# Gated linear attention and a spatial gating unit on one core: keys and queries of three batches turned on VectorE and placed through HBM

## The chip, the cores and the metric

The kernel runs on one core of one Trainium2 chip. The metric is the device time in microseconds of one execution. The engines are TensorE (PE, with its weight loads PEld), VectorE (DVE), ScalarE (ACT), GpSimd (POOL) and SyncE (SP), which issues all the transfers of this kernel in one queue, in order.

## The reference

For 4 batches, 8 heads, 768 steps and head dimension 48, gated linear attention keeps a state per head. Its output, heads side by side (width 384), is the input of a gated MLP with a spatial gating unit:

```
f = sigmoid(f_logit)
for t in range(768):
    state = f[t][:, None] * state + outer(k[t], v[t])
    y[t] = q[t] @ state
h = gelu_tanh(x @ w_in)            # x = y, 384 -> 1024
u, v = split(h)                    # 512 each
v_n = (v - mean) / sqrt(var + 1e-6) * g_ln
v_s = w_sg @ v_n + b_sg            # over the 768 steps
out = x + (u * v_s) @ w_out        # 512 -> 384
```

All in float32.

## The kernel before, in words

The 768 steps of a batch are cut into 6 tiles of 128 steps (24 tiles over all, `N`, numbered n; batch 0 is tiles 0 to 5), and a tile into two chunks of 64. Within a chunk attention is done by products, between chunks by the state.

The steps of one tile are named in the kernel by a short name and the tile's number:

- `f`, `k`, `q`, `v`: loads, 192 KB each. Keys and queries go to `kqs` (three buffers), each head padded from 48 to 64 columns (`HD`), so that two heads stand at partitions 0 and 64 after a transpose.
- `e`, `l`, `lh`, `ll`, `cum`, `up`, `dn`: the gates' logarithms, their running sums by a matmul, and the exponentials of both signs. `mq` and `mk` multiply queries and keys with them (L529, L525) on VectorE or GpSimd.
- `do`, `di`: the decay of a whole chunk is brought to columns; for tiles 6 and up by way of a scratch in HBM, `dec_d` (L532, L536).
- `tr`: eight TensorE transposes (L559), one for each pair of heads of keys and of queries, into two PSUM banks; `tc` copies them to `sks` (two buffers), on ScalarE as a rule (L566, recorded at the helper's line L321).
- `su`: score products (L578) and state products keys x values (L583); `ms` masks the scores into `sts` (L588); `sa`, `sm` add to the state and decay it (L604, L607).
- `y`: output products (L626), masked scores with values and queries with the state; `ty`, `jy` take them out (L630, L634).
- `xT`: transposes of the attention's output (L655), `xh`, `xl` split it into a high and a low float32r part. `hv`, `hu`, `sg`, `po` are the matmuls of the MLP, all recorded at L650, each product as three float32r matmuls.

`su` and `y` use the array in quadrants (64 x 64), the others the whole array.

The order on all engines is written out ahead by a planner (`Plan`): a greedy schedule with a cost for each step (`T`), a queue and wire time for each transfer (`W`), rings of buffers (`RINGS`), due times for TensorE's steps, and a list of shifts of due times and choices of engine (`MOVES`). The due times lay the attention of batch b among the spatial gating and projection of batch b - 1, between the fractions `A0` and `A1` of that work; in batch 0 they follow the arrival of the loads. `op`, `pe` and `dma` add a step with what it needs. Up to 45 us the planner fills TensorE's gaps with matmuls of zeros (L992).

Of the kernel before, what the change touches and what calls it, by code (L numbers as in the profile page):

```python
# [64 lines left out]
cs:-20.3 wain0:23.1 wfin0:0:POOL wfin1:0:POOL wfin2:0:DVE wbin3:74.5 wcin3:-16 wrin4:6 wcin4:-2.5 wdin4:248.6  # L65
wfin4:0:POOL ldin5:-27.6 ldin6:19.5 wfin6:55.2 ldin7:-0.2 wrin7:-173.7 wdin7:-33.2 ldout0:1.4 wpout0:8.4 wdout0:-20.4
ldout1:102.8 waout1:-4.7 wl0.1:734.5 ldsg1:15.1 wl1.0:243.5 wT1.1:-1.1 ldsg2:1.8 wT3.0:-1.8 wT4.0:172.6 wl4.0:-28.9
wT4.1:25.4 ldsg5:-33.2 wT5.0:-378.9 v0:2.1 w0.0:0:POOL mk0:0:POOL sz0:-389.4 sa0.0:-15.5 nl0:435.6 po0:292 f1:-417.7
k1:-526.9 q1:-48.1 w1.0:0:POOL w1.1:0:POOL do1:-7.7 ms1:-73.4 sa1.0:-14.4 sm1.0:0:POOL hv1:322.3 ns1:41 nl1:4.4
f2:-1.5 k2:8.6 v2:110.2 w2.0:0:POOL w2.1:-23.4 mq2:-141.7 di2:0:ACT tc2.0:-20.1 tc2.1:-3.7 ms2:-0.6 xl2:-8.7  # L70
sg0.0:84.4 sm_0.0:27.1 hu0.1:-291 sm_0.2:0:POOL gu0.3:-6 sg0.3:153.3 sb0.3:18.6 sm_0.3:0:POOL mq3:-138.3 sm3.0:0:POOL
y3:5.2 po3:746.4 f4:31.3 tc4.0:0:DVE sm4.0:-216.6 sm4.1:0:POOL q5:1.6 w5.0:-108.7 w5.1:-57.1 dn5:244.4 mk5:0:POOL
su5:-1.6 ms5:-0.3 sm5.0:0:POOL sm_1.0:0:POOL hu1.1:6.3 hu1.2:-0.2 gu1.2:-85 hu1.3:391.7 sm_1.3:0:POOL w6.1:-178.4
dn6:140.6 mk6:0:POOL sm6.1:0:POOL xT6:-11.5 k7:-2.9 ll7:145.8 up7:0.7 mq7:0:POOL mk7:0:POOL tc7.0:0:DVE xT7:-40.9
nd7:25 po7:995.4 ll8:-42:POOL mq8:-53.5:POOL xT8:-25.9 hv8:-20.6 sg2.2:34.6 mq9:0:POOL y9:-1 po9:951.5 lh10:-86.2
ll10:0:POOL y10:-287.3 f11:52.3 tc11.1:0:DVE hv11:66.2 sg3.0:1549 sg3.1:1637.5 sg3.3:10.9 po11:59.2 dn13:6.1
mq14:0:POOL mk14:0:POOL tr14:9.8 sm14.1:41.5 hv14:103.6 hu4.1:99.7 sg4.2:188 po14:645.7 f15:-2.9 lh15:-38.6
tc15.1:0:DVE po15:14.5 f17:-49.9 lh17:-27.7 mq17:0:POOL tr17:-130.7 hu5.0:-128.5 sg5.0:1269.4 sg5.1:150.6
sm_5.1:0:POOL sg5.2:295.4 po17:945.8 cum18:-26.7 up18:35.6 mq18:0:POOL y18:-129.1 ty18:-18.6 ll19:0:POOL mq19:0:POOL
# [212 lines left out]
def gla_moe_kernel(ctx: ExitStack, tc: tile.TileContext, q, k, v, f, w_in, g_ln, w_sg, b_sg, w_out, cst, out):  # L292
# [230 lines left out]
    def mul_k(n, e):  # L523
        kt = kqs[n % NQ][:, 0, :, 0:D]
        ENG[e].tensor_mul(kt, kt, f_raw.pop(n))  # L525

    def mul_q(n, e):
        qt = kqs[n % NQ][:, 1, :, 0:D]
        ENG[e].tensor_mul(qt, qt, eb_of[n][:, :, 0:D])  # L529
# [41 lines left out]
    def scores(n):  # L571

        kq, sk, vs = kqs[n % NQ], sks[n % NS], vss[n % NV]
        last = n % NT == NT - 1
        for p in range(NP):
            for par, c in ((0, 0), (1, 1), (0, 1), (1, 0)):
                r = feat(par)
                nc.tensor.matmul(ps_s[rows(score_rows(c, 2 * p + par)), par, p * C : (p + 1) * C], sk[r, 0, p, c], sk[r, 1, p, c], start=True, stop=True)  # L578
            for c, par in ((0, 0), (1, 1), (0, 1), (1, 0)):
                if c == 1 and last:  # L580
                    continue
                h = 2 * p + par
                nc.tensor.matmul(  # L583
                    ps_s[rows(par), c, 256 + p * D : 256 + (p + 1) * D], kq[rows(c), 0, h, :], vs[rows(c), h], start=True, stop=True
                )
# [523 lines left out]
```

## Time and profile before

| | |
|---|---|
| time, three runs | 382.89, 384.6 (median), 385.07 us |
| span of the profiled execution | 380.6 us |
| own time of the profiled execution | not on the page; the runs are 2.3 to 4.5 us above its span |
| instructions | 11390 |
| TensorE busy | 369.6 us (97%), 4808 matmuls |
| weight loads busy | 341.5 us (90%) |
| VectorE busy | 233.6 us (61%) |
| ScalarE busy | 213.2 us (56%) |
| GpSimd busy | 55.9 us (15%) |
| DMA queue of the program | 31.35 MB in 123476 packets, 39.8% of 16 engines' span |
| eight transposes of a tile (L559) | 273 ns median each, pipelined |

A span runs from the first instruction to the last; the time is some microseconds longer. Busy time counts an engine's instructions; matmuls are pipelined, so TensorE's busy time does not say that it is at its peak. The chain of work that ended last is followed back from the last instruction through what released it. A wait is put down to what came last of all that an instruction needed.

### The profile page before, as it was taken

The page shows a single profiled execution, that of the slowest core. Times are in us where ns is not written, and L with a number is a line of the kernel's source. Part 1 is how long each engine was busy: PE and PEld are TensorE (multiplying, and loading weights), DVE is VectorE, ACT ScalarE, POOL GpSimd, SP SyncE. Part 2 cuts the span into 40 slices and gives each one's busy share as a digit, 9 for nine tenths or more (in the row PEclk, how much of TensorE's full clock was granted, in tenths as well). Part 3 has the DMA queues.
Part 4 walks back from the last instruction along what each step waited for, and adds up shares of the span by engine and source line. Part 5 has one row for each costly group of instructions (what it writes and reads, how often), then busy time and mean ns, then how long its engine had stood idle before and what let it go on. Part 6 is the DMA issues. An engine that isn't in the chain of part 4 may idle for free.

```text
span 380.6 us, 11390 instructions
## 1 busy us (share of the span) xinstructions
PE 369.6 (97%) x4808; PEld 341.5 (90%) x4808; DVE 233.6 (61%) x544; ACT 213.2 (56%) x483; POOL 55.9 (15%) x97
## 2 busy tenths in 40 slices
PE   8999999999999999999999999999989999999992
PEld 3777988999998898999999998999979998999991
DVE  3599998689578764247769635266656644254531
ACT  4677769637565957647447647678343554811100
POOL 1211453012341011100201110132000100200000
PEclk9999999999999999999999999999999999999998
DMA  8989998200285951002476622012244110000021
GB/s 178 219 231 233 223 215 202 72 14 0 45 145 90 198 99 22 22 21 39 94 144 109 106 66 41 22 21 45 44 106 85 22 46 2 2 21 2 0 83 49
DMA packets 123533, 32.13 MB, mean 84 GB/s; under 512 B 115797, under 2 KB 122069, under 8 KB 123477
## 3 DMA queue, kind: packets, MB, share of 16 engines
q1 hardware_dynamic: 123476, 31.35, 39.8%
q8 instruction: 39, 0.64, 0.8%
q14 instruction: 18, 0.14, 0.1%
HBM read 26.57 MB, written 4.77 MB: 82 GB/s over the span
## 4 chain that ended last, share of the span: by engine, by line
PE 96%; DMA 1%; DVE 1%; ACT 0%; issue 0%; SPq 0%
PE ps_b L650 67%; PE ps_y L626 6%; PE ps_b L559 6%; PE ps_s L578 4%; PE ps_b L992 3%; PE ps_s L583 2%; PE ps_b L655 2%; PE ps_b L508 1%; PE ps_b L444 1%; PE ps_b L511 1%; PE ps_b L544 1%; DMA gg<-in_moe_w_in_dram 1%; PE ps_b L512 1%; DVE tmp L768 0%; ACT u L393 0%
## 5 line engine op out<-in xcount | busy, mean ns | idle before, releaser
L650 PE MATMUL ps_b<-w_sg_hi,vh 128*128 128x384 f32 x192 | 65.3, 340 | 0.0
L650 PE MATMUL ps_b<-w_sg_hi,vh_lo 128*128 128x384 f32 x192 | 64.9, 338 | 0.0
L650 PE MATMUL ps_b<-w_sg_lo,vh 128*128 128x384 f32 x192 | 64.8, 338 | 0.0
L650 PE MATMUL ps_b<-w_out_hi,gg 128*128 128x384 f32 x174 | 48.0, 338 | 0.0
L737 DVE SCALAR_TENSOR_TENSOR tmp<-ps_b,cols,b_bc 128x384 f32<-128x384 f32 x32 | 19.7, 615 | 29.5 <-PE ps_b L650 25.0
L650 PEld LDWEIGHTS ps_b<-w_sg_hi,vh 128*128 128x128 f32 x192 | 36.1, 188 | 0.2
L650 PEld LDWEIGHTS ps_b<-w_sg_lo,vh 128*128 128x128 f32 x192 | 36.1, 188 | 0.0
L650 PEld LDWEIGHTS ps_b<-w_sg_hi,vh_lo 128*128 128x128 f32 x192 | 36.0, 188 | 0.0
L321 ACT COPY sk<-ps_b 112x512 f32<-112x512 f32 x44 | 24.6, 589 | 14.2 <-PE ps_b L559 8.0
L650 PEld LDWEIGHTS ps_b<-w_out_hi,gg 128*128 128x128 f32 x174 | 31.8, 188 | 0.1
L650 PE MATMUL ps_b<-xTh,w_in_hi 128*128 128x384 f32 x84 | 29.2, 348 | 0.0
L650 PE MATMUL ps_b<-w_out_lo,gg 128*128 128x384 f32 x87 | 29.1, 335 | 0.0
L710 DVE SCALAR_TENSOR_TENSOR vh_lo<-vg,vg_rs,vh 128x512 fp32r<-128x512 f32 x24 | 18.0, 749 | 17.1 <-ACT vh L705 17.1
L650 PE MATMUL ps_b<-xTl,w_in_hi 128*128 128x384 f32 x84 | 28.4, 338 | 0.0
L650 PE MATMUL ps_b<-xTh,w_in_lo 128*128 128x384 f32 x84 | 28.4, 338 | 0.0
L753 ACT CAST gg<-tmp 128x384 fp32r<-128x384 f32 x29 | 14.5, 510 | 23.3 <-DVE tmp L742 20.6
L316 ACT ACTIVATE f<-f 128x384 f32<-128x384 f32 x48 | 24.8, 524 | 4.6 <-DMA f<-in_f_logit_dram 4.1
L559 PE MATMUL ps_b<-cs,kq 128*112 128x128 f32 x192 | 25.5, 275 | 1.9 <-DVE kq L525 1.5
L626 PE MATMUL ps_y<-vs,st 64*64 64x48 f32 x768 | 27.2, 219 | 0.0
L626 PE MATMUL ps_y<-S,sk 48*64 48x48 f32 x768 | 27.0, 219 | 0.0
L626 PEld LDWEIGHTS ps_y<-vs,st 64*64 64x64 f32 x768 | 24.7, 134 | 2.0 <-issue 1.4
L650 PE MATMUL ps_b<-w_in_hi,xTh 128*128 128x512 f32 x63 | 26.2, 416 | 0.0
...
## 6 DMA issues: line engine op xcount, KB each, us to landing
f<-in_f_logit_dram SPq DMA_DIRECT2D x24, 192.0 KB, 3.7
kq<-in_k_dram SPq DMA_DIRECT2D x24, 192.0 KB, 4.0
kq<-in_q_dram SPq DMA_DIRECT2D x24, 192.0 KB, 5.9
vs<-in_v_dram SPq DMA_DIRECT2D x24, 192.0 KB, 4.5
out_dram<-tmp SPq DMA_DIRECT2D x24, 192.0 KB, 1.9
...
```

Of the source, the lines that this page charges most:

```text
L316: nc.scalar.activation(dst, src, func, **kw)
L321: (nc.scalar.copy if e == "ACT" else ENG[e].tensor_copy)(dst, src)
L559: nc.tensor.transpose(psum[f"tr{n}"][j][:W2, p * P : (p + 1) * P], kq[:, j, 2 * p : 2 * p + 2, :].rearrange("t h d -> t (h d)")[:, :W2], i ...
L578: nc.tensor.matmul(ps_s[rows(score_rows(c, 2 * p + par)), par, p * C : (p + 1) * C], sk[r, 0, p, c], sk[r, 1, p, c], start=True, stop=True)
L583: nc.tensor.matmul(ps_s[rows(par), c, 256 + p * D : 256 + (p + 1) * D], kq[rows(c), 0, h, :], vs[rows(c), h], start=True, stop=True)
L626: nc.tensor.matmul(ps_y[rows(c), half, h * D : (h + 1) * D], a, m, start=start, stop=stop)
L650: nc.tensor.matmul(ps, a, m, start=(j == 0), stop=(j == len(seq) - 1))
L655: nc.tensor.transpose(ps[:, j], x_sb[n][:, j * P : (j + 1) * P], ident)
L710: nc.vector.scalar_tensor_tensor(vl, v_raw.pop(n), rs, vh.bitcast(F32), op0=ALU.mult, op1=ALU.subtract)
L737: nc.vector.scalar_tensor_tensor(t, psum[f"sg{g}.{ft}"][:, :E], g_col[:, ft : ft + 1], b_bc[:, tokens(g)], op0=ALU.mult, op1=ALU.add)
L753: nc.scalar.copy(gt[(g, ft)][0], g_raw[(g, ft)])
L992: steps = plan.warm(plan.run(), 45.0, lambda k, n: nc.tensor.matmul(ps_b[k][:, : n * P], zeros, zeros[:, None, :].to_broadcast((P, n, P)), ...
```

## The change

For batches 1 to 3 (tiles 6 to 23) `tr` and `tc` go. In their place:

- `tt`, three for each tile: VectorE turns 32 x 32 blocks of the scaled keys and queries (`turn_kq`), 128 steps x 8 (key or query, pair of heads) x 32 columns, and writes 8 values side by side for each time.
- `to`, three for each tile: a store of 128 KB to a scratch in HBM, `kq_d`, pieces of 1 KB (`turned_out`).
- `ti`, two for each tile: a read of 192 KB back to 48 partitions each, 4 KB to a partition (`turned_in`).

Keys and queries of these tiles are stored without the padding. The layout of `sks` is the same for all tiles now, [feature, time, key or query, pair], so that neighbouring times are 8 values apart; batch 0 keeps `tr` and `tc`, and the copy writes in this layout. The state products of all tiles load 48 columns of the keys and not 64; the rows between are cleared once (`zs`). `sts` has one buffer, not two, so that `ms` needs `y` of the tile before. `y` stands ahead of the next tile's `su` in the due times, and `A0`, `A1` and `MOVES` are others.

```diff
+BL = 32
+NBL = 2 * D // BL
-A0, A1 = 0.25, 0.75
+A0, A1 = 0.1, 0.8
...
-    sks = [cp.tile([P, 2, NP, 2, C], F32, name=f"sk{i}") for i in range(NS)]
-    sts = [cp.tile([P, 2, NP, C], F32, name=f"st{i}") for i in range(NS)]
+    sks = [cp.tile([P, P, 2, NP], F32, name=f"sk{i}") for i in range(NS)]
+    sts = [cp.tile([P, 2, NP, C], F32, name="st")]
...
+    kq_d = dp.tile([N, 2, D, P // BL, BL, 2 * NP], F32, name="kq_d")
...
+    def kq_of(n):
+        t = kqs[n % NQ]
+        if n < NT:
+            return t[:, :, :, 0:D]
+        return t.rearrange("t j h d -> t (j h d)")[:, : 2 * E].rearrange("t (j h d) -> t j h d", j=2, d=D)
...
     def trans_copy(n, j, e):
-        copy(e, sks[n % NS][:W2, j].rearrange("d p c t -> d (p c t)"), psum[f"tr{n}"][j][:W2])
+        copy(e, sks[n % NS][:W2, :, j].rearrange("d t p -> d p t"), psum[f"tr{n}"][j][:W2].rearrange("d (p t) -> d p t", p=NP))
+    def turn_kq(n, m):
+        t = tt_of[n, m] = buf("tt", [P, BL, 2 * NP], F32)
+        blocks = kq_of(n).rearrange("t j (p x) d -> t (j p) (x d)", x=2)[:, :, m * BL : (m + 1) * BL]
+        nc.vector.transpose(t.rearrange("r t a -> r a t"), blocks)
+    def turned_out(n, m, e):
+        dst = kq_d[n].rearrange("x d b t a -> (x d) b (t a)")[m * BL : (m + 1) * BL].rearrange("r b y -> b r y")
+        ENG[e].dma_start(dst, tt_of.pop((n, m)).rearrange("r t a -> r (t a)"))
+    def turned_in(n, par, e):
+        ENG[e].dma_start(sks[n % NS][feat(par)].rearrange("d t j p -> d (t j p)"), kq_d[n, par].rearrange("d b t a -> d (b t a)"))
...
-                nc.tensor.matmul(ps_s[rows(score_rows(c, 2 * p + par)), par, p * C : (p + 1) * C], sk[r, 0, p, c], sk[r, 1, p, c], start=True, stop=True)
+                nc.tensor.matmul(ps_s[rows(score_rows(c, 2 * p + par)), par, p * C : (p + 1) * C], sk[r, rows(c), 0, p], sk[r, rows(c), 1, p], start=True, stop=True)
...
-                    ps_s[rows(par), c, 256 + p * D : 256 + (p + 1) * D], kq[rows(c), 0, h, :], vs[rows(c), h], start=True, stop=True
+                    ps_s[feat(par), c, 256 + p * D : 256 + (p + 1) * D], kt[rows(c), h], vs[rows(c), h], start=True, stop=True
...
-                b_ = (sk[feat(par), 1, p, c], Sn[feat(par), c, p])
+                b_ = (sk[feat(par), rows(c), 1, p], Sn[feat(par), c, p])
...
-                att.append([f"su{m0 + i}"] + ([f"y{m0 + i - 1}"] if i else []) + ([f"tr{m0 + i + 1}"] if i + 1 < NT else []) + ([f"xT{m0 + i - 2}"] if 2 <= i < 2 + GR else []))
+                att.append(([f"y{m0 + i - 1}"] if i else []) + [f"su{m0 + i}"] + ([f"xT{m0 + i - 2}"] if 2 <= i < 2 + GR else []))
...
-            dma(f"{'kq'[j]}{n}", lambda e, n=n, j=j: load_kq(n, j, e), W["kq"[j]], ["clear", f"tr{n - NQ}", f"su{n - NQ}"])
+            dma(f"{'kq'[j]}{n}", lambda e, n=n, j=j: load_kq(n, j, e), W["kq"[j]], ["clear", f"tr{n - NQ}", f"su{n - NQ}"] + [f"tt{n - NQ}.{m}" for m in range(NBL)])
...
+        if early:
             pe(f"tr{n}", ...)
             ...
+        else:
+            for m in range(NBL):
+                op(f"tt{n}.{m}", lambda e, n=n, m=m: turn_kq(n, m), T["tt"], [f"mq{n}", f"mk{n}"], take=("tt",))
+                dma(f"to{n}.{m}", lambda e, n=n, m=m: turned_out(n, m, e), W["to"], [f"tt{n}.{m}"], free=[("tt", f"tt{n}.{m}", 0)])
+            for par in range(2):
+                dma(f"ti{n}.{par}", lambda e, n=n, par=par: turned_in(n, par, e), W["ti"], [f"to{n}.{m}" for m in range(par, par + 2)] + [f"su{n - NS}", f"y{n - NS}"])
-        op(f"ms{n}", lambda e, n=n: mask_scores(n), T["ms"], [f"su{n}", f"y{n - NS}"])
+        op(f"ms{n}", lambda e, n=n: mask_scores(n), T["ms"], [f"su{n}", f"y{n - 1}"])
```

More of the change, by code (lines that the diff above doesn't have):

```diff
@@ L36 @@
 CW = 128 + 128 + 64
-A0, A1 = 0.25, 0.75
+BL = 32
+NBL = 2 * D // BL
+A0, A1 = 0.1, 0.8
 T_FIRST, T_TILE, V_FIRST, V_TILE, T_SG = 16, 8, 22, 3.589, 43.931
 T = dict(
-    cum_c="DVE:0.2", clear="POOL:1.3", zy="DVE:0.6", wa="ACT:0.452", wb="DVE:0.268", wp="DVE:0.268", wq="DVE:0.468", wr="DVE:0.268", wc="DVE:0.468",
+    cum_c="DVE:0.2", clear="POOL:1.3", zy="DVE:0.6", zs="DVE:0.35", wa="ACT:0.452", wb="DVE:0.268", wp="DVE:0.268", wq="DVE:0.468", wr="DVE:0.268", wc="DVE:0.468",
     wd="DVE:0.468 POOL:1.0", we="ACT:0.403", wf="DVE:0.468 POOL:1.0", wh="ACT:0.362", wl="DVE:0.465", e="ACT:0.507", l="ACT:0.413",
@@ L64 @@
 MOVES = """
[L65 to L79, printed above, removed]
@@ L80 @@
-xT20:40 sg6.1:373.3 sg6.3:178.9 f21:-165.8 q21:158.4 w21.1:0:POOL xT21:-24.3 f22:-19.9 lh23:-172.2 ll23:0:POOL
-tr23:-429.2 sg7.1:48.1 hu7.2:-22.7 ok_s:683.9
+cs:-120.7 wdin0:287.6 wpin1:191.3 wdin1:-92.1:DVE wfin1:-77.8 wbin2:124.3 wdin2:366.9:DVE wfin2:0:POOL wbin3:515.4
+wdin4:-2.6:DVE ldin5:-396 ldin6:-63 wpin7:36 wdin7:5.6 wfin7:-97.2 wpout0:26.9 wdout0:-120.2:POOL waout1:136.4
+wpout1:-13.5 wdout1:3:POOL ldout2:-6.7 wrout2:0.9 wdout2:4.4 wfout2:-0.3:DVE wbout3:205.3 wcout3:80.9 wT0.0:-126.2
@@ new lines @@
+wh0.0:-328.1 wT0.1:147.4 ldsg1:4.4 wh1.0:-33.2 wT1.1:27.9 wT3.0:-96.6 wl3.0:102.9 ldsg5:102.8 wh5.1:-16.8
+w0.0:31.4:DVE w0.1:0:POOL mk0:1.6:POOL tc0.1:-31.6 sa0.0:3 sa0.1:202.6 xl0:78.4 po0:88.3 f1:-116.5 k1:-1185.7
+q1:-181.7 w1.0:-20.4 w1.1:34.2:DVE mk1:82.4:POOL di1:210.8 tc1.1:118.6:ACT ms1:-15.2 sm1.0:6.3:POOL ns1:-44.8 nl1:82.7
+f2:-5.6 w2.0:1.6 w2.1:-37.4 tc2.0:24.6 ms2:194.5 sm2.0:-1:DVE xl2:18.5 hv2:-106.5 hu0.0:-35.6 gu0.0:6.7 sm_0.0:-254.7
+sh0.0:-58.1 sg0.2:-39.3 hu0.3:-189.4 sb0.3:-43.2 sm_0.3:-241.8 w3.0:120.9 di3:0:ACT sa3.0:13.7 sa3.1:4.5 sm3.1:17.6
@@ new lines @@
+nq3:102 re3:-4.9 w4.0:44.5:DVE w4.1:15.2:DVE up4:-1.3 mq4:-25.1:DVE mk4:-4.2:DVE di4:-3.2 tc4.0:3.5:DVE tc4.1:118.9
+su4:-41.9 sa4.0:340.7 sm4.1:158.2 nh4:3.7 po4:-99.4 w5.1:1.3 cum5:12.5 mk5:250:DVE di5:-15.9:ACT ms5:70 sb1.0:297.5
+sm_1.0:-1.2:POOL sg1.1:72.9 sb1.1:-249.2 sm_1.1:36.1:POOL hu1.2:-177.8 sb1.2:178.3 sm_1.2:524.8 hu1.3:81.1 out5:18.7
+w6.0:-1.8:POOL lh6:0.4 mq6:-17.8:DVE mk6:28.7:POOL tt6.1:106 sa6.1:115.2 sm6.1:0:POOL w7.1:-122.2:POOL lh7:-109.9
+mq7:-202.8:DVE mk7:0:DVE tt7.0:54.1 tt7.1:-19.2 sm7.0:-14.7:DVE po7:859.3 w8.0:0:POOL w8.1:-15.6:DVE lh8:-257.5:ACT
@@ new lines @@
+mq8:-92.6:POOL mk8:0:POOL tt8.0:288.6 sa8.1:136 y8:137.4 jy8:23.1 sg2.1:123.2 sm_2.1:12.8 sl2.1:-42 sm_2.2:-505.6
+k9:-178.8 w9.0:-22.5 lh9:9.3 ll9:0:POOL to9.1:-3 sm9.0:-11.6 v10:-57.1 ll10:-67.4:DVE mq10:40.6 po10:221.2 f11:-64.1
+lh11:-75.6 ll11:-42.9:DVE mq11:-47.5 su11:-812.4 sm11.0:-35.4 sg3.0:1698.4 sg3.1:1877.7 sg3.3:75.6 w12.1:-23.7
+lh12:1.1:ACT w13.0:0:POOL lh13:0.8:DVE ll13:188.8:POOL mq13:135.3:POOL su13:0.7 sa13.0:21.3 ty13:4.9 xh13:0.2
+out13:2.5 w14.0:-123.7 lh14:8.5:DVE mq14:0.1:POOL mk14:30 tt14.1:-37.3 to14.2:63.3 hu4.1:313.1 sm_4.1:-16.2 gu4.2:-0.7
@@ new lines @@
+sb4.3:67 sl4.3:-106.4 po14:207.5 f15:8.6 ll15:189.9 mk15:-22.8:DVE di15.0:-0.1 tt15.1:53.4 w16.0:-7.4:POOL w16.1:155.9
+lh16:-73.8 ll16:126.4:DVE sm16.0:-19.5 y16:152.6 lh17:5.2:ACT ll17:-0.9 mq17:-31.8 tt17.1:-8.2 sg5.0:1142.6
+sm_5.0:123.9 sg5.1:-81.1 sm_5.1:-36.4:POOL sg5.2:692 hu5.3:-6.1 f18:-41.9 ll18:-1.2 mq18:0:DVE mk18:6.3:DVE mq19:-9.3
+ms19:-0.4 sm19.1:96.8:POOL hv19:430.1 ll20:41.3:POOL mq20:28.9 mk20:65.5:POOL su20:0.4 sm20.1:-11.3 jy20:-30.5
+xT20:89.4 hu6.0:137.4 sb6.0:19.3 sm_6.1:1.4 sg6.2:138.3 po20:-4.1 f21:290.5 lh21:0:DVE ll21:10.8:DVE
@@ L82 @@
+sm21.0:-228.3:POOL ty21:-0.5 nr21:-0.1 w22.0:1.8 lh22:0:ACT sm22.0:-7.7:DVE f23:-180.7 q23:4.4 w23.1:-32.9
+lh23:-4.2:ACT ll23:0:POOL do23:-111.8 di23.0:52.5 tt23.1:49.7 to23.1:-19.8 nh23:-10.7 sm_7.1:-94.6 sh7.3:-0.6
 """
@@ L523, in mul_k @@
     def mul_k(n, e):
[L524 removed]
+        kt = kq_of(n)[:, 0]
         ENG[e].tensor_mul(kt, kt, f_raw.pop(n))
     def mul_q(n, e):
[L528 removed]
+        qt = kq_of(n)[:, 1]
         ENG[e].tensor_mul(qt, qt, eb_of[n][:, :, 0:D])
@@ L875, in gla_moe_kernel @@
     op("zy", lambda e: nc.vector.memset(ps_y[:, :, 0:E], 0.0), T["zy"], ())
+    op("zs", lambda e: nc.vector.memset(ps_s[:, :, 256 : 256 + NP * D], 0.0), T["zs"], ())
     for kind, m in (("in", 8), ("out", 4)):
```

25 lines of the change are left out of this document (13 added, 12 removed).

## The prediction

> **What bounds the kernel now.** First the page's busy times and its chain of work that ended last.
>
> ```profile
> span 380.6 us, 11390 instructions
> PE 369.6 (97%) x4808; PEld 341.5 (90%) x4808; DVE 233.6 (61%) x544; ACT 213.2 (56%) x483; POOL 55.9 (15%) x97
> ...
> PE 96%; DMA 1%; DVE 1%; ACT 0%; issue 0%; SPq 0%
> PE ps_b L650 67%; PE ps_y L626 6%; PE ps_b L559 6%; PE ps_s L578 4%; PE ps_b L992 3%; PE ps_s L583 2%; PE ps_b L655 2%; PE ps_b L508 1%; PE ps_b L444 1%; PE ps_b L511 1%; PE ps_b L544 1%; DMA gg<-in_moe_w_in_dram 1%; PE ps_b L512 1%; DVE tmp L768 0%; ACT u L393 0%
> ```
>
> The chain lies on TensorE for 96% of the span; the transposes of keys and queries (L559) are 6% of it. An average hides stages, so second the busy times by stage: batch 0 with the weights up to 95 us, then one row for each of batches 1 to 3 (us, then PE, PEld, DVE, ACT, POOL, granted clock, DMA share, GB/s).
>
> ```profile
> 0.00:95.00 95.00, 92.91 (x1185) 79.16 (x1186) 76.72 (x191) 65.55 (x152) 23.21 (x41) 1.00 0.72 159
> 95.00:173.00 78.00, 78.00 (x1128) 73.29 (x1128) 46.44 (x107) 49.82 (x114) 14.09 (x22) 1.00 0.41 78
> 173.00:251.00 78.00, 78.00 (x1128) 73.47 (x1128) 45.88 (x108) 48.12 (x110) 7.73 (x16) 1.00 0.41 76
> 251.00:330.00 79.00, 77.46 (x1124) 72.64 (x1123) 44.68 (x101) 42.79 (x96) 10.16 (x16) 1.00 0.23 45
> ```
>
> In batches 1 to 3 TensorE is busy without a gap, at the full granted clock, while VectorE and ScalarE are some 60% busy and DMA 41% or less. So a microsecond of TensorE work removed there is a microsecond of time, as long as nothing else becomes late. Third, what TensorE waits for in the whole run (total, times, longest):
>
> ```profile
> PE ps_b L559 <- DVE kq L525: 1.5, 1, 1.5
> ...
> PEld ps_s L578 <- issue: 3.2, 15, 0.4
> PEld ps_b L559 <- DVE kq L525: 2.0, 1, 2.0
> ```
>
> One late operand of a transpose, 1.5 us, and otherwise almost nothing. Fourth, the chain in order of time within batch 1 (start, us, what), which prices one tile.
>
> ```profile
> by line: PE ps_b L650 71.7%; PE ps_y L626 7.9%; PE ps_b L559 7.1%; PE ps_s L578 4.7%; PE ps_s L583 3.0%; PE ps_b L655 2.5%; PE ps_b L511 1.9%; PE ps_b L512 1.4%
> ...
> 100.25 0.87 PE ps_b L559 x8
> ...
> 101.48 3.16 PE ps_b L650 x18
> 104.64 0.28 PE ps_s L578 x8
> ...
> 118.61 0.93 PE ps_y L626 x64
> 119.55 1.02 PE ps_b L559 x8
> ...
> 122.66 0.33 PE ps_b L655 x3
> ...
> 128.79 0.87 PE ps_b L559 x8
> 129.66 1.08 PE ps_y L626 x64
> 130.74 0.13 PE ps_s L578 x8
> ...
> 131.67 3.87 PE ps_b L650 x18
> ```
>
> A tile's eight transposes cost 0.87 us; the score and state products (L578, L583) 0.93 us (130.74 to 131.67); the output products (L626) 0.93 us. The 0.15 us more at 119.55 and at 129.66 is paid by whatever comes first after a switch between small and full matmuls. It stays with the neighbours, because the new order has as many visits to the small products (output of the last tile and scores of the next side by side) as the old one.
>
> **The change part by part.**
>
> *Transposes removed.* 18 tiles x 0.87 us = 15.7 us of TensorE, all in the stages without a gap. Check: 7.1% of 78 us is 5.5 us in batch 1, six tiles at 0.92, the excess being the switches. Gain taken 15.7, ends 14.2 (0.79 a tile, if the 0.08 at the end of a group also stays) and 16.6. The single 1.5 us wait belonged to such a transpose; its late key product is next needed by the VectorE turn, so I count no gain from it.
>
> *State products load 48 columns.* In the 0.93 us of scores each of four array quadrants takes 16 weight loads of 64 columns, 58 ns each; the transposes of x (L655) take 0.33 us for three loads of 128 columns, 110 ns each. The line through both gives 45 ns for 48 columns, so 13 ns x 8 loads = 0.10 us a tile. Batches 1 to 3 have 15 full tiles and three with half the state products: 16.5 x 0.10 = 1.7 us. Batch 0's 0.6 us I leave out, since TensorE still waits for loads and runs filler matmuls (L992) there. Ends: 0, if the pace of 128 instructions in 0.93 us binds rather than the columns, and 2.3.
>
> *The turned tile is read with a stride.* Its layout goes from time innermost to eight values between neighbouring times, 32 bytes apart, for all 24 tiles. Half of the weight loads of the scores and half of those of the outputs read it so: 16 loads per quadrant and tile. The trace of before has no such read by TensorE. Lower end: nothing. Upper end: a strided load takes as long as one of twice the columns, 110 ns for 58, or 52 ns x 16 = 0.83 us a tile, 14.9 us over 18 tiles and 19.8 over 24. The nearest rows are two reads by ScalarE, of every second word and of a contiguous tile:
>
> ```profile
> L321 ACT COPY sk<-ps_b 112x512 f32<-112x512 f32 x44 | 24.6, 589 | 14.2 <-PE ps_b L559 8.0 <-PE ps_y L626 3.1 <-PE ps_s L578 3.0
> ...
> L604 DVE TENSOR_TENSOR S<-S,ps_s 112x192 f32<-112x192 f32 x40 | 14.0, 349 | 7.4 <-PE ps_s L583 6.4 <-POOL S L607 0.4
> ...
> L753 ACT CAST gg<-tmp 128x384 fp32r<-128x384 f32 x29 | 14.5, 510 | 23.3 <-DVE tmp L742 20.6 <-PE ps_b L650 1.7 <-DVE u L414 0.7
> ...
> L529 DVE TENSOR_TENSOR kq<-kq,eb 128x384 f32<-128x384 f32 x17 | 10.5, 615 | 1.9 <-ACT eb L316 1.1 <-DMA kq<-in_q_dram 0.7
> ...
> L393 ACT ACTIVATE u<-gg 128x384 f32<-128x384 f32 x12 | 6.6, 558 | 3.8 <-DMA gg<-in_moe_w_out_dram 1.6 <-DVE w_out_lo L435 1.5 <-DMA gg<-in_moe_w_in_dram 0.7
> ```
>
> The strided one (L393) takes 558 ns, the contiguous cast (L753) 510: a tenth. Also, a stream of 18 matmuls of 384 columns passes in 3.16 us, 0.46 ns a column, while a weight load takes 0.9 ns a column: it asks for data at half the pace that the memory meets there. By these I take 0 and keep 19.8 as the other end. This is the largest unknown.
>
> [...]
>
> *The turn on VectorE.* Three instructions a tile, 54, each 128x256. Between 349 ns (192 columns) and 615 ns (384) lies 440; strided writing could raise it to the 680 of twice the length. Taken 450 ns: 24 us, 8 per batch. VectorE goes from 46 of 78 us to 54 of 73: cover enough, but its queue is fuller; a late chunk of the gating or of the low parts would hold TensorE. ScalarE loses up to 36 copies of 0.59 us, 21 us off the path. In batch 0 its copies write with the stride: at most double, 0.6 us in each tile's path, which lies beside the loads (DMA share 0.72 in that stage): taken 0.
>
> *The scratch.* Nearest rows: the round trip of the decays through HBM and the output stores.
>
> ```profile
> f<-in_f_logit_dram SPq DMA_DIRECT2D x24, 192.0 KB, 3.7
> ...
> kq<-in_q_dram SPq DMA_DIRECT2D x24, 192.0 KB, 5.9
> ...
> out_dram<-tmp SPq DMA_DIRECT2D x24, 192.0 KB, 1.9
> ...
> dec<-dec_d SPq DMA_DIRECT2D x36, 1.5 KB, 2.4
> ...
> L536 SPq DMA_DIRECT2D dec<-dec_d x36: 303/463/1517, 97.8 to 292.4; - x36
> L532 SPq DMA_DIRECT2D dec_d<-eb x18: 488/503/690, 96.1 to 289.1; - x18
> ```
>
> Three stores of 128 KB and two reads of 192 KB a tile, in pieces of 1 and 4 KB: 90 issues on SP x 0.46 = 41 us, 14 a batch beside 48 issues (some 23 us) already there, so SP is half busy. Path of a tile: turns 1.3 us, last store 2.4 to land, second read 0.5 to issue and 2.4 to land: 6.6 us, where transposes and two copies took 0.9 + 1.1 = 2.0. The 4.6 us more are hidden by tiles in flight: a turned tile is refilled after the output products two tiles back, and from the end of those at 119.5 to the next scores but one at 130.74 there are 11 us for the 3 us of the reads. If that cover goes, TensorE stands in program order and all of it is paid. On SP, behind a read that waits for its stores, stand the loads of later tiles (three buffers deep) and output stores (the pool tmp, three deep, which VectorE waits for). With 18 tiles I take 2.0 us of new TensorE waits, about one more like the late key product seen above; ends 0 and 18 (1 us a tile).
>
> *Sum.* 380.6 - 15.7 - 1.7 + 2.0 = 365.2 us of span. The page gives the execution's span alone; the three runs, 382.89 to 385.07 with median 384.6, put 2.3 to 4.5 us around it, 4.0 for the median. So 369 us, 4% less.
>
> **Rivals.**
>
> *Strided weight loads run at half pace.* Place: L578 and the half of L626 with the turned queries. Price 0.83 us a tile for 18 tiles and about three of batch 0 after its fillers: 17.4 us, so 386.6, up to 389 with all 24. It decides from 46 ns a load (17.4 us spread over 24 x 16), where the gain is gone. For: nothing in the trace shows such a read free. Against: 8 bytes cost a tenth at most, and the load's slow pace. It is the one that can end slower. Chance 0.22, of which slower 0.13, within 0.5% 0.06, faster 0.03. [...]
>
> *Turned tiles late.* The loads take 3.7 to 5.9 us to land, and stores of a scratch queued behind them could take as long, twice in a row: 10 us and more instead of 6.6, with SP in order. Half of the tiles waiting 1 us costs 9 us: about 376, range 373 to 384. For: a fuller SP and VectorE. Against: DMA at 41%, stores landing in 1.9. Chance 0.16: faster 0.15, slower 0.01.
>
> *The freed TensorE time isn't used:* gating and scratch set the pace of a batch, and the time stays at 384. Against: some 50 of the 78 us of a batch are L650, much of it sums of the batch before that wait for no new tile. Chance 0.04: faster 0.01, within 0.5% 0.03.
>
> **How the numbers follow.** Mine has 0.58, with its own range of 365 to 374 (waits 0 to 7; the columns 0 to 2.3). Below 364 would need no wait and every term at its upper end: 0.04. Above 384 lies most of the first rival, 0.15. So 364 to 384 leaves out 0.19. About 0.5%, 1.9 us, is what a measurement of this kernel can tell from no change: faster 0.58 + 0.03 + 0.15 + 0.01 = 0.77, within it 0.06 + 0.03 = 0.09, slower 0.13 + 0.01 = 0.14.
>
> **What would show it.** No L559 after 95 us, and each stage of a batch down from 78 to some 73 us at equal L650. The score and state products at 0.83 us where they were 0.93, outputs still 0.93; with a stride that costs, up to 1.25 and 1.35, and the weight loads of L578 longer than those of L583. Turns near 450 ns, VectorE near 54 us a batch. Waits of TensorE's first score load for the turned tile adding to some 2 us. I am wrong if the products are slower, if those waits pass 6 us, or if batch 0 ends later than 95 us.

## The result and the profile after

The changed kernel takes 427.96 us (median of four runs, 425.44 to 429.79) where the kernel before takes 384.35 beside it: 1.1155 times as long, interval 1.1101 to 1.1209, or 43.6 us more. The forecast was 369, 4% less. The spans of the profiled executions are 423.7 and 380.6 us.

The page of the changed kernel: span, busy times, and the chain that ended last by engine and by line. L592 is the turn, L596 the store to the scratch, L599 its read; L683, L611, L616, L659 and L688 are what L650, L578, L583, L626 and L655 were. In the other kernels below these lines are one or two further up or down.

```profile
span 423.7 us, 11257 instructions
...
PE 393.6 (93%) x4668; PEld 359.4 (85%) x4668; DVE 261.5 (62%) x603; ACT 202.3 (48%) x450; POOL 47.1 (11%) x92
...
PE 57%; DMA 21%; DVE 11%; ACT 6%; issue 3%; SPq 2%; POOL 0%; DVEq 0%; POOLq 0%
PE ps_b L683 40%; DMA kq_d<-tt 9%; PE ps_y L659 5%; PE ps_s L611 5%; DMA kq<-in_k_dram 3%; DMA sk<-kq_d 3%; DVE tt L592 3%; DMA vs<-in_v_dram 3%; ACT f L326 2%; DMA kq<-in_q_dram 2%; DVE kq L547 1%; PE ps_b L688 1%; ACT sk L331 1%; PE ps_s L616 1%; PE ps_b L577 1%
```

The chain was 96% TensorE and is 57%; DMA has gone from 1% to 21%, the store of the turned tile alone to 9%. Yet TensorE is also busy for 24.0 us longer (393.6 against 369.6) with 140 matmuls fewer. So two things have happened: its work has become longer, and it waits. Its busy times by stage (us, then PE, PEld, DVE, ACT, POOL, granted clock, DMA share, GB/s), batch 0 and then one row for each of batches 1 to 3, show both:

```profile
0.00:95.00 95.00, 90.81 (x1136) 76.30 (x1137) 73.07 (x178) 72.31 (x155) 15.68 (x36) 1.00 0.74 159
95.00:185.00 90.00, 79.78 (x1051) 72.43 (x1051) 54.66 (x129) 35.43 (x81) 11.69 (x19) 0.96 0.57 120
185.00:280.00 95.00, 87.75 (x1113) 81.88 (x1112) 58.23 (x132) 41.54 (x96) 8.05 (x16) 0.98 0.56 114
280.00:372.00 92.00, 88.57 (x1111) 83.13 (x1110) 54.70 (x122) 41.37 (x95) 9.48 (x16) 0.96 0.39 90
```

A batch takes 90 to 95 us where it took 78 to 79, TensorE is idle for 20.9 us of the three stages (277 less 256.1) where it was 1.5, and the granted clock, which was 1.00, is 0.96 to 0.98.

The longer work, in the chain in order of time inside batch 2 (start, us, what):

```profile
256.00 1.57 PE ps_y L659 x44
257.57 0.30 PE ps_s L611 x8
257.88 0.09 PE ps_s L616 x8
...
259.03 0.09 PE ps_s L616 x8
```

The output products of a tile take 1.57 us and took 0.93. One of the four pairs of heads needs 0.29 us for scores and 0.09 for state products, so the four need 1.55 us (257.57 to 259.12), where before it was 0.93, fewer columns in the state products included. Together that is 1.26 us a tile. Of the 16 weight loads of a quadrant in 1.57 us, eight are still contiguous; at the 58 ns that they took before, (1.57 - 8 x 0.058) / 8 leaves 138 ns for one strided load. This is an estimate; the scores, with two strided loads a quadrant in 0.29 us, give 145.

The waits: TensorE's two longest for data and two of VectorE's, each with total, times and longest; the last line is of the kernel before.

```profile
PEld ps_s L611 <- DMA sk<-kq_d: 13.2, 10, 3.3
...
PEld ps_b L688 <- DVE x L667: 4.5, 3, 2.4
...
DVE vs L331 <- DMA vs<-in_v_dram: 20.7, 11, 3.5
...
DVE tt L592 <- DMA kq_d<-tt: 9.3, 11, 2.8
```

```profile
DVE vs L321 <- DMA vs<-in_v_dram: 7.6, 9, 2.0
```

The scores wait 13.2 us for turned tiles. VectorE waits 9.3 us for the stores to free the turn's buffers, and 20.7 us for the loads of the values, which stand behind the stores in SP's queue (7.6 us before). VectorE is idle for more than a third of the time, and the experiments show that this last wait costs little by itself (`spread` below still has 18.1 us of it). One late tile, followed in the chain and then, microsecond by microsecond, in the busy times (columns as above):

```profile
294.68 1.69 DVE tt L592 x3
...
296.63 5.22 DMA kq_d<-tt
301.87 2.95 DMA sk<-kq_d
...
306.76 5.48 PE ps_b L683 x18
```

```profile
297.00:298.00 1.00, 1.00 (x8) 1.00 (x6) 0.68 (x2) 0.89 (x3) 0.00 (x0) 1.00 0.24 81
298.00:299.00 1.00, 1.00 (x7) 1.00 (x7) 0.74 (x2) 0.66 (x2) 0.00 (x0) 1.00 0.42 82
299.00:300.00 1.00, 1.00 (x8) 1.00 (x7) 0.91 (x2) 0.03 (x1) 0.00 (x0) 1.00 0.35 95
...
302.00:303.00 1.00, 0.00 (x0) 0.00 (x0) 0.97 (x3) 1.00 (x3) 0.14 (x1) 1.00 0.63 168
303.00:304.00 1.00, 0.49 (x2) 0.31 (x2) 0.22 (x1) 0.57 (x2) 1.00 (x1) 1.00 0.82 210
304.00:305.00 1.00, 0.14 (x5) 0.14 (x8) 0.00 (x0) 0.00 (x0) 0.08 (x1) 0.78 0.86 133
305.00:306.00 1.00, 1.00 (x42) 1.00 (x44) 0.00 (x0) 0.00 (x0) 0.00 (x0) 0.50 0.00 0
```

The turns end at 296.37, and the first score follows at 304.86. In between the stores drain for 5.22 us, in the rows shown at 81 to 95 GB/s with a quarter to two fifths of the DMA engines' time used, then the reads take 2.95 us, with 0.63 to 0.86 of it in use. TensorE is idle for 2.4 of the three microseconds from 302 to 305, and is then granted half the clock: the next 18 matmuls of 384 columns take 5.48 us where the same 18 took 3.16.

### The profile page after: what moved, and what is told of

Read it like the earlier page. It is cut to its first block, busy times and chain, and to the rows that moved or that the text cites. A ratio compares the mean times of both kernels' runs of the same rounds, so it can differ in the third digit from the quotient of the medians.

```text
span 423.7 us, 11257 instructions
## 1 busy us (share of the span) xinstructions
PE 393.6 (93%) x4668; PEld 359.4 (85%) x4668; DVE 261.5 (62%) x603; ACT 202.3 (48%) x450; POOL 47.1 (11%) x92
## 4 chain that ended last, share of the span: by engine, by line
PE 57%; DMA 21%; DVE 11%; ACT 6%; issue 3%; SPq 2%; POOL 0%; DVEq 0%; POOLq 0%
PE ps_b L683 40%; DMA kq_d<-tt 9%; PE ps_y L659 5%; PE ps_s L611 5%; DMA kq<-in_k_dram 3%; DMA sk<-kq_d 3%; DVE tt L592 3%; DMA vs<-in_v_dram 3%; ACT f L326 2%; DMA kq<-in_q_dram 2%; DVE kq L547 1%; PE ps_b L688 1%; ACT sk L331 1%; PE ps_s L616 1%; PE ps_b L577 1%
## 5 line engine op out<-in xcount | busy, mean ns | idle before, releaser
L683 PE MATMUL ps_b<-w_sg_hi,vh 128*128 128x384 f32 x192 | 67.7, 353 | 0.4 <-DVE tmp L770 0.4
L683 PE MATMUL ps_b<-w_sg_lo,vh 128*128 128x384 f32 x192 | 66.6, 347 | 0.0
L683 PE MATMUL ps_b<-w_sg_hi,vh_lo 128*128 128x384 f32 x192 | 66.3, 345 | 0.0
L611 PE MATMUL ps_s<-sk 48*64 48x64 f32 x768 | 42.9, 319 | 13.1 <-DMA sk<-kq_d 10.6
L611 PEld LDWEIGHTS ps_s<-sk 48*64 48x64 f32 x768 | 36.0, 206 | 17.9 <-DMA sk<-kq_d 13.2
L683 PE MATMUL ps_b<-w_out_hi,gg 128*128 128x384 f32 x174 | 48.5, 341 | 0.5 <-DVE tmp L801 0.5
L659 PEld LDWEIGHTS ps_y<-vs,st 64*64 64x64 f32 x768 | 35.3, 138 | 5.7 <-issue 4.0
L659 PE MATMUL ps_y<-vs,st 64*64 64x48 f32 x768 | 39.6, 220 | 0.1
L659 PE MATMUL ps_y<-S,sk 48*64 48x48 f32 x768 | 39.2, 283 | 0.0
L683 PEld LDWEIGHTS ps_b<-w_sg_hi,vh 128*128 128x128 f32 x192 | 37.5, 195 | 1.2 <-DVE tmp L770 0.8
L592 DVE STREAM_TRANSPOSE tt<-kq 128x256 f32<-128x256 f32 x54 | 32.1, 666 | 9.4 <-DMA kq_d<-tt 9.3
L683 PEld LDWEIGHTS ps_b<-w_sg_lo,vh 128*128 128x128 f32 x192 | 37.5, 195 | 0.0
L683 PEld LDWEIGHTS ps_b<-w_sg_hi,vh_lo 128*128 128x128 f32 x192 | 37.4, 195 | 0.0
L659 PEld LDWEIGHTS ps_y<-S,sk 48*64 48x64 f32 x768 | 36.1, 208 | 0.0
L326 ACT ACTIVATE f<-f 128x384 f32<-128x384 f32 x48 | 24.6, 521 | 19.7 <-DMA f<-in_f_logit_dram 19.4
L683 PEld LDWEIGHTS ps_b<-w_out_hi,gg 128*128 128x128 f32 x174 | 31.7, 188 | 1.0 <-issue 0.6
L616 PE MATMUL ps_s<-vs,kq 64*48 64x48 f32 x704 | 31.4, 220 | 0.0
L683 PE MATMUL ps_b<-w_out_lo,gg 128*128 128x384 f32 x87 | 29.1, 335 | 0.0
L683 PE MATMUL ps_b<-xTh,w_in_hi 128*128 128x384 f32 x84 | 29.1, 346 | 0.0
L683 PE MATMUL ps_b<-xTl,w_in_hi 128*128 128x384 f32 x84 | 28.4, 338 | 0.0
```

The lines of the kernel that those rows point to most:

```text
L326: nc.scalar.activation(dst, src, func, **kw)
L592: nc.vector.transpose(t.rearrange("r t a -> r a t"), blocks)
L616: nc.tensor.matmul(ps_s[feat(par), c, 256 + p * D : 256 + (p + 1) * D], kt[rows(c), h], vs[rows(c), h], start=True, stop=True)
L659: nc.tensor.matmul(ps_y[rows(c), half, h * D : (h + 1) * D], a, m, start=start, stop=stop)
L683: nc.tensor.matmul(ps, a, m, start=(j == 0), stop=(j == len(seq) - 1))
```

## The experiments

In the diffs of this section long index expressions are shortened to `...` or to words.

Two theories stood at first. S: the strided reads by TensorE are the loss. L: the late turned tiles are. Later ones came from what these two left over.

**Each suspect alone.** The kernel before, with only the layout of the turned tile changed:

```diff
-    sks = [cp.tile([P, 2, NP, 2, C], F32, name=f"sk{i}") for i in range(NS)]
+    sks = [cp.tile([P, P, 2, NP], F32, name=f"sk{i}") for i in range(NS)]
...
-  copy(e, sks[n % NS][:W2, j]..., psum[f"tr{n}"][j][:W2])
+  copy(e, sks[n % NS][:W2, :, j]..., psum[f"tr{n}"][j][:W2]...)
...
-  sk[r, 0, p, c], sk[r, 1, p, c]      # scores; sk[feat(par), 1, p, c] in the outputs
+  sk[r, rows(c), 0, p], sk[r, rows(c), 1, p]      # sk[feat(par), rows(c), 1, p]
```

> The kernel before with nothing but the new layout of the turned tile: eight values between neighbouring times, written by the copies of the transposes and read by the score and output products. Transposes, order and transfers stay. Theory S (the strided weight loads are most of the loss): in the changed kernel the scores of a tile took 1.53 us for 0.93 and the outputs 1.57 for 0.93, so 1.24 us a tile; over 24 tiles 29.8, of which some 4 beside the filler matmuls of batch 0: about 410 us (405 to 415). Theory L (the loss is the late scratch, and strided loads hide behind other work when nothing is late): 384 to 390.

Measured 411.08 us, 1.0733 times the time before (1.0686 to 1.0780): 28 us from the layout alone. Its weight loads of scores and outputs and ScalarE's copies (min/median/max ns):

```profile
L578 PEld LDWEIGHTS ps_s<-sk x768: 191/213/217, 17.0 to 341.8; 48*64 48x64 f32 x192
...
L626 PEld LDWEIGHTS ps_y<-S,sk x768: 191/213/220, 21.7 to 347.1; 48*64 48x64 f32 x192
...
L321 ACT COPY sk<-ps_b x44: 1067/1169/1259, 11.7 to 333.1; 112x512 f32<-112x512 f32 x44
```

Before, the loads' medians were 133 and 135 ns and that of the copies 587. 24 tiles x 1.26 us are 30.2 us: the layout costs about what the rows say. The copies are slower too, but it is TensorE's work that lengthens the run: the span is 408.2 us for 380.6, and from 95 to 372 us TensorE is busy for 276.4 of 277 us, at a granted clock of 1.00.

Three kernels undo parts of the change instead. `contig` lets TensorE read the bytes of the turned tile contiguously, with the same traffic. `nowait` fills the turned tile from the input of the queries, in reads of the same size, so that no read waits for a store. `contig_nowait` has both. All three, and every kernel made from `contig_nowait`, compute with other values than the ones meant and show times alone.

```diff
+  skv = sk.rearrange("d t j p -> d (t j p)").rearrange("d (j p c t) -> d j p c t", ...)      # contig
-  sk[r, rows(c), 0, p], sk[r, rows(c), 1, p]
+  skv[r, 0, p, c], skv[r, 1, p, c]
...
-  ENG[e].dma_start(sks[n % NS][feat(par)]..., kq_d[n, par]...)                              # nowait
+  ENG[e].dma_start(sks[n % NS][feat(par)]..., q flat, 48 rows of 1024 values)
```

> The changed kernel, where the score and output products read the same bytes of the turned tile as runs of 64 neighbouring values; these are other values than the ones meant, so this shows times alone. Everything else, the strided writing and the scratch too, as in the changed kernel. Theory S: scores 0.88 us and outputs 0.93 a tile again, 30 us less: about 398 us, or a little lower, since tiles then wait for the scratch more. Theory L: TensorE waits for the tiles anyway, and the time saved turns into waits: 420 to 428.

> The changed kernel, where the two reads into the turned tile fetch as many bytes of the query input and not of the scratch, so they don't wait for the stores; turns and stores are still made. The turned values are then not the ones meant. Theory L: the waits of score products for the turned tile go, and with them most of the 19 us of idle TensorE and the 9 us of lower granted clock: about 400 us. Theory S: lateness costs little by itself: 415 to 428.

> Both at once: contiguous reads of the turned tile by TensorE and reads that don't wait for the scratch; the values are other ones. If strided loads and late tiles are the whole of the loss, what is left is the removal of the transposes as forecast: 366 to 375 us. If it stays above 385, there is a third cost (VectorE's turns, SP's queue, the order of the work).

Measured: `contig` 418.64 us (1.0945, 1.0894 to 1.0997), `nowait` 423.62 (1.1061, 1.1013 to 1.1109), `contig_nowait` 413.28 (1.0804, 1.0744 to 1.0864). S and L each predicted far more than the 9.3 and 4.3 us that came back (8.0 and 3.6 by the ratios, since the kernel before took 382.63 us beside these). Both mended together left 30.7 us above that, where the prediction's gain was expected if they were the whole loss. The waits of `contig_nowait` (TensorE's, then VectorE's):

```profile
PEld ps_s L612 <- DMA sk<-in_q_dram: 14.3, 10, 3.8
PEld ps_b L690 <- DVE x L669: 6.9, 5, 3.7
...
DVE vs L331 <- DMA vs<-in_v_dram: 20.4, 11, 3.7
...
DVE tt L592 <- DMA kq_d<-tt: 9.8, 11, 2.1
```

The reads no longer wait for stores by semaphore and are nearly as late as before: 14.3 us of waits where `contig` has 16.2, and 11.7 in `nowait` where the changed kernel has 13.2. What remains in common is the traffic. When TensorE's work got shorter, part of the time became idle time, since the tiles come no earlier: in the same 277 us, from 95 to 372, TensorE is idle for 30.7 us in `contig` and for 20.9 in the changed kernel.

**Taking the scratch away step by step.** Theory Q is that the scratch's own traffic holds up everything in SP's queue. From `contig_nowait`, `no_store` issues no store, `no_dma` no read either, `no_turn` no turn either.

```diff
-  ENG[e].dma_start(dst, tt_of.pop((n, m)).rearrange("r t a -> r (t a)"))      # no_store
+  tt_of.pop((n, m), None)
...
-  ENG[e].dma_start(sks[n % NS][feat(par)]..., q...)                          # no_dma, too
+  pass
...
-  nc.vector.transpose(t.rearrange("r t a -> r a t"), blocks)                 # no_turn, too
```

> The last kernel (contiguous reads by TensorE, turned tile filled from the query input) without the stores to the scratch; VectorE still turns. Values are other ones. Theory Q (the third cost is the transfers: stores take SP's queue and the DMA engines from the loads, and VectorE's turns stand in its queue until a store has freed one of three buffers): 385 to 395 from 413. Theory V (VectorE is late by the turns' own 0.67 us x 54): within 5 us of 413. Theory O (the written order itself is loose, made for other durations): within 5 us of 413.

> The same without stores and without the reads into the turned tile, which keeps what batch 0 left in it. VectorE still turns, TensorE does all its products. Theory Q: all transfers as before the change, so 368 to 375. Theory V: still above 395. Theory O: still above 395.

> The same without the turns as well: only what the change removes and its order are left. Theory V: falls by 15 or more against the kernel without scratch transfers, to some 370. Theory Q: 0 to 3 lower than that kernel, 366 to 372. Theory O: stays above 385.

Measured: `no_store` 376.18 us (0.9819, 0.9785 to 0.9852), `no_dma` 371.31 (0.9697, 0.9664 to 0.9730), `no_turn` 368.66 (0.9623, 0.9591 to 0.9656). The stores are worth 37.1 us, the reads 4.9, the turns 2.7. The same 73 us from the start of batch 1 of `contig_nowait`, then of `no_store` (columns as in the stages above, then TensorE's waits for the turned tiles of `no_store`):

```profile
95.00:168.00 73.00, 61.24 (x977) 55.41 (x976) 46.91 (x113) 25.75 (x57) 7.69 (x13) 0.91 0.64 139
```

```profile
95.00:168.00 73.00, 70.03 (x1056) 63.99 (x1056) 51.33 (x124) 37.95 (x85) 10.43 (x19) 1.00 0.56 112
```

```profile
PEld ps_s L612 <- DMA sk<-in_q_dram: 2.5, 5, 0.8
```

Without stores TensorE is busy for 70 of 73 us and not 61, at the full clock and not 0.91. The reads of both kernels need nothing from the stores, and still TensorE waits for them for 14.3 us with the stores and 2.5 us without: what is issued behind the stores comes late. `no_turn` is also the measure of the gains: without transposes, with 48 columns and the new order, and nothing in the transposes' place, it is 14.1 us below its 382.7 before. The new order, with its one `sts` buffer, is thus not a loss by itself.

**What of the stores?** `store_const` takes the bytes from a tile of constants, so that a store waits for no turn. `store_kq` takes them from the keys and queries. `store_small` stores a sixteenth of the bytes in as many stores. `state48` is the other part of the change by itself, on the kernel before.

```diff
-  ENG[e].dma_start(dst, tt_of.pop((n, m))...)                          # from contig_nowait
+  ENG[e].dma_start(dst, b_bc[:, 0 : BL * 2 * NP])                      # store_const
+  ENG[e].dma_start(dst, kq_of(n) flat[:, m * 256 : (m + 1) * 256])     # store_kq
+  ENG[e].dma_start(dst[:, :, 0:16], tt flat[:, 0:16])                  # store_small
...
-  ps_s[rows(par), ...], kq[rows(c), 0, h, :], vs[rows(c), h]           # state48, from before
+  ps_s[feat(par), ...], kq[rows(c), 0, h, 0:D], vs[rows(c), h]
```

> The kernel with contiguous reads and the turned tile filled from the query input (413.3 us with its stores, 376.2 without). Its stores have the same size, place and target, but take their bytes from a constant tile, so they wait for no turn and no turn waits for them; the scratch holds other values. Theory R (the turns stand in VectorE's queue until a store has landed and freed one of three buffers, and all behind them is late): 376 to 383. Theory H (SP's queue stands at a store until its turn is done, and loads behind it are late): 376 to 383 too. Theory B (the bytes and the issues of the stores themselves delay the loads): 400 to 413.

> The same with stores that take their bytes from the scaled keys and queries before the turn: SP still waits for the multiplications ahead of the turn, and the next load but two into that buffer waits for the store, but no turn waits for a store. The scratch holds other values. Theory R: 376 to 385. Theory H: 395 to 413. Theory B: 400 to 413.

> The same with stores of the turned tile itself, waits and buffers as in the changed kernel, but a sixteenth of the bytes: 64 B of each 1 KB piece, as many pieces. Theory B: 376 to 385. Theory H: 395 to 413. Theory R: the small store lands sooner, 2 us where the full one took 3 to 5, so between: 385 to 400.

> The kernel before, where the state products load 48 columns of the keys and not 64, with the rows between cleared once; all else as before. By the line through weight loads of 64 and 128 columns: 0.10 us a tile, 1.7 us in batches 1 to 3, so 382.6 where before is 384.3 (-0.45%), and up to 2.3. From the changed kernel, whose state products stand at 0.09 us for eight where they were 0.10: 0.05 us a tile, 1 us. If the pace of the instructions binds: no change.

Measured: `store_const` 404.16 us (1.0573, 1.0523 to 1.0623), `store_kq` 402.29 to 408.01 (1.0569, 1.0480 to 1.0659), `store_small` 386.48 (1.0108, 1.0071 to 1.0144). Where the bytes come from and what a store waits for is worth 9 us at most, where theories R and H needed 30 or more from `store_const`; a sixteenth of the bytes in the same 54 issues gives back 27. (386.48 lies just above the range of theory B and in that of R, which `store_const` and `store_kq` rule out.) So it is mainly the moving of the bytes that costs. `state48` took 381.69 us (0.9969, 0.9943 to 0.9995): 1.0 us less. Its loads of the state products, with those of the kernel before above them:

```profile
L583 PEld LDWEIGHTS ps_s<-vs,kq x704: 133/134/135, 17.6 to 315.6; 64*64 64x64 f32 x176
```

```profile
L583 PEld LDWEIGHTS ps_s<-vs,kq x704: 122/122/123, 16.4 to 314.0; 64*48 64x48 f32 x176
```

**Why do 128 KB move so slowly?** The store's target has the outer dimension four (blocks of 32 times), then 32 rows, then 1 KB. The fine rows above show a quarter to two fifths of 16 engines in use. Theory E: such a store is spread over few DMA engines. `spread` gives the stores of `contig_nowait` a linear target of 128 rows of 1 KB. `spread_real` gives it to the changed kernel, which keeps its strides and needs four reads a tile for two. `bmajor` keeps four by 32 by 1 KB but lets each group of 32 rows be one run of 32 KB, so that only the addresses differ.

```diff
-    kq_d = dp.tile([N, 2, D, P // BL, BL, 2 * NP], F32, name="kq_d")
+    kq_d = dp.tile([N, NBL, P, BL * 2 * NP], F32, name="kq_d")         # spread, spread_real
+    kq_d = dp.tile([N, P // BL, 2 * D, BL * 2 * NP], F32, name="kq_d") # bmajor
...
-  ENG[e].dma_start(dst, tt...)                                        # dst: b, r, y
+  ENG[e].dma_start(kq_d[n, m], tt...)                                 # spread, spread_real
+  ENG[e].dma_start(kq_d[n][:, m * BL : (m + 1) * BL], tt...)          # bmajor
```

> The kernel with contiguous reads and the turned tile filled from the query input (413.3 us; 376.2 without stores, 386.5 with a sixteenth of their bytes). Only the target of the stores changes: the 128 pieces of 1 KB of a store lie one behind the other and not in a 4 x 32 grid of steps. Theory E (a store is dealt out by its outer dimension of four, so it runs on about 4 of the 16 DMA engines, at 80 to 97 GB/s and a DMA share of 0.24 to 0.42, and all that is queued on those engines waits): 380 to 390. Theory B (the bytes written as such): 405 to 413.

> The changed kernel with that target for its stores and the reads arranged to match: four reads a tile and not two, in pieces of 1 KB, with the right values and the strided layout. Theory E: the late tiles and the low granted clock go, the strided loads stay: 376 + 30 = 406, 398 to 410. Theory B: 420 to 428.

> As the kernel with contiguous reads and the turned tile filled from the query input (413.3 us), with another target of the stores: four runs of 32 KB, one for each block of 32 steps, so the addresses of neighbouring pieces follow on each other, but the transfer still has the dimensions 4 x 32 x 1 KB. If a store is dealt out to the engines by its outer dimension of four: 405 to 416, bursts at 80 to 97 GB/s again. If it was the pitch of 4 KB between neighbouring pieces in HBM: 382 to 392, as with the linear target.

Measured: `spread` 388.28 us (1.0126, 1.0055 to 1.0197), 25 below `contig_nowait`; `spread_real` 407.42 (1.0635, 1.0602 to 1.0669), 20.5 below the changed kernel; `bmajor` 413.33 (1.0789, 1.0737 to 1.0841), the same as `contig_nowait`. `spread` moves the same bytes as `contig_nowait`, so it is not their number that costs 25 us but how the transfer is cut; the 12 us between `spread` and `no_store` (376.18) were not taken apart. Two microseconds during three stores of `bmajor`, then two of `spread_real` (the same columns):

```profile
286.00:287.00 1.00, 1.00 (x7) 1.00 (x7) 0.42 (x2) 0.98 (x4) 0.00 (x0) 1.00 0.27 93
287.00:288.00 1.00, 1.00 (x8) 1.00 (x7) 1.00 (x2) 0.35 (x1) 0.00 (x0) 1.00 0.43 88
```

```profile
285.00:286.00 1.00, 1.00 (x8) 1.00 (x7) 1.00 (x4) 0.00 (x0) 0.00 (x0) 1.00 0.85 254
286.00:287.00 1.00, 1.00 (x7) 1.00 (x6) 0.54 (x2) 0.96 (x4) 0.00 (x0) 1.00 0.58 199
```

With the outer dimension four the stores moved some 90 GB/s at a share of 0.24 to 0.43, in both layouts of the addresses; with 128 rows outermost, 199 to 254 at 0.58 to 0.85. The lowest shares during such stores, 0.24 in the changed kernel and 0.27 in `bmajor`, are the time of about four of the 16 engines (3.8 and 4.3, an estimate), which would fit theory E; in the higher ones, up to 0.43, other transfers issued meanwhile may be included, and no view here counts the engines of a single store.

**The stride's size, and both mended.** `stride8_only` lays the turned tile of the kernel before out in pairs, so that neighbouring times are 8 bytes apart. `fixed` is the changed kernel with that layout and the linear target; its four reads a tile come in pieces of 256 B.

```diff
+    sks = [cp.tile([P, NP, P, 2], F32, name=f"sk{i}") for i in range(NS)]   # both
+  sk[r, p // 2, rows(c), p % 2], sk[r, 2 + p // 2, rows(c), p % 2]
...
+    kq_d = dp.tile([N, NBL, P, BL * 2 * NP], F32, name="kq_d")              # fixed
+  t = tt_of[n, m] = buf("tt", [P, NP, BL, 2], F32)
+  ENG[e].dma_start(sks[n % NS][f0 : f0 + k_]..., kq_d[n, m] as r, g, b, (t x))   # four a tile
```

> The kernel before with a turned tile of pairs: neighbouring times are two values, 8 bytes, apart and not eight values as in the first of these experiments (411.1 us). [...] If every stride costs a weight load the same: 405 to 411. If the cost goes with the span of bytes read: 388 to 396.

> The changed kernel with both: stores spread over the engines, and the turned tile in pairs (8 bytes between times), filled in pieces of 256 B by four reads a tile. Right values. Theory E and a free stride of 8 bytes: transposes gone, 372 to 386, below or about the kernel before; what is above 369 are waits for the scratch and the smaller pieces. If the pieces of 256 B make the reads late: 386 to 400.

Measured: `stride8_only` 384.45 us (1.0036, 1.0009 to 1.0062), 1.5 us above its own before and below the ranges of a cost for every stride (405 to 411) and of a cost by the span of bytes (388 to 396), with the loads and copies

```profile
L578 PEld LDWEIGHTS ps_s<-sk x768: 132/135/141, 17.8 to 317.2; 48*64 48x64 f32 x192
...
L321 ACT COPY sk<-ps_b x44: 601/627/666, 13.0 to 309.2; 112x512 f32<-112x512 f32 x44
```

A stride of 8 bytes cost TensorE next to nothing: the loads of scores and outputs have medians of 135 ns, where they were 133 and 135, and their matmuls 228 and 220, where they were 225 and 218. One of 32 more than doubled the time between loads (58 to 138 ns, by the estimate above). `fixed` took 405.14 us (1.0582, 1.0507 to 1.0657), above both expectations: its loads have their old durations (medians 135 ns), and its tiles are late again. The issues of its reads and TensorE's first wait:

```profile
L601 SPq DMA_DIRECT2D sk<-kq_d x72: 557/603/2072, 92.0 to 336.2; - x72
```

```profile
PEld ps_s L613 <- DMA sk<-kq_d: 11.3, 9, 2.7
```

72 reads at 603 ns hold SP's queue for 43 us, where the changed kernel's 36 held it for some 13 at 353; and they come in pieces of 256 B (145460 packets under 512 B in the run, 117812 in `spread_real`). `spread_real` has as many reads in pieces of 1 KB, at 417 ns, and waits 4.4 us for them, but its longer products leave them more time. Which of these makes the tiles of `fixed` late was not tried apart.

## Why the prediction was wrong, and where it was right

- *Transposes and 48 columns* (17.4 us): right in kind, somewhat too high. `no_turn` gives 14.1 for them with the order; 1.0 of it are the columns (`state48`) and not 1.7, which leaves 13.1 for the transposes, below their lower end of 14.2. That the 368.66 us of `no_turn` meet the forecast's 369 is partly luck, since its kernel before took 382.7 us and not 384.6, and the sum had 2.0 us of waits that it hasn't. What was wrong by tens of microseconds is all in what takes the transposes' place.
- *"The turned tile is read with a stride ... I take 0"*: the first step that failed. The rows that led to 0 were of a stride of 8 bytes, and `stride8_only` shows that such a stride cost TensorE hardly anything either (loads of 135 ns, as before): these rows could not speak about 32 bytes. The other argument, that a weight load asks for data at half the pace of a matmul, is refuted by 58 ns becoming 138. The upper end was also too low, 0.83 us a tile against 1.26 (and 24 x 0.83 is 19.9, not 19.8), since it took a strided load for one of twice the columns (110 ns). The first rival had the place right and priced it at 17.4 to 19.8 us; alone it is worth 28. Two strides were tried, 8 bytes at a median duration of 135 ns and 32 at 213; where between them the cost begins no run here shows.
- *"Last store 2.4 to land"*: the second step that failed. It was taken from the decays of 1.5 KB, beside output stores of 192 KB at 1.9 us. The output stores have 128 rows outermost; the scratch's stores have four, and three in a row take 5.22 and elsewhere 5.59 us. With 128 rows outermost the same stores land in 2.8 us (median, `spread_real`). The packets' length was looked at and the outer dimension was not. The second rival named late tiles and even the stores as their cause, but priced them at 9 us: it counted a wait of 1 us in half of the tiles, not that what is issued behind the stores is late too (37 us between `contig_nowait` and `no_store`), nor that TensorE was granted half the clock after such a wait (0.50 from 305 to 306 us).
- *New waits on TensorE, 2.0, ends 0 and 18*: measured 19.4 more idle us in the three batches, just beyond the upper end, and by the lower clock some 9 more (an estimate: 0.04 x 90, 0.02 x 95 and 0.04 x 92).
- *The cover of 11 us for a tile's path*: the path was 1.7 us of turns, 5.2 of stores and 3.0 of reads, 10 us and not 6.6, and with the queue's delay the cover was gone.
- *VectorE's turns at 450 ns*: measured 666 as a mean, near the 680 named for strided writing; in `fixed`, which writes at 8 bytes, the median is 428. Hidden, as forecast (2.7 us for all, `no_turn` against `no_dma`).
- *The rivals as alternatives*: both came true at once. Their prices don't add up, and neither is recovered alone: mending the reads gave 9.3 us, the wait 4.3, the stores' target 20.5. While tiles are late TensorE's longer work fits partly into its waits, and a shorter one turns into more of them.

The sum by the traces of before and after: -15.7 for transposes, 24 x 1.26 = +30.2 for the products with strided reads and fewer columns, +19.4 idle, +9 by the clock: +42.9 beside the 43.1 us of span. TensorE's own times say the same, 24.0 us more busy and 19.1 more idle. This is an account by rows; the experiments bear out the signs and the order of its terms, not each figure.

One rival stays untested. The written order reckons 0.37 us on the wire for a store (`W`, `to`), while 128 KB at 90 GB/s take some 1.5, and 0.33 us for a turn (`T`, `tt`), while three take 1.69. So it asks for the reads earlier than they can come. How much an order planned with the measured costs would win back was not tried.

Of all versions that do the whole computation, `state48`, the kernel before with 48 columns, is the only one below the kernel before, by 0.3%. The gain of 14 us shows with nothing in the transposes' place. To keep it takes a way to turn the tiles that leaves neighbouring times 8 bytes apart, as in `stride8_only`, and doesn't make the transfers late; none of these versions has both.
